# A linear attention followed by two Strassen MLPs: a new instruction order, and the ninth key block's products on half-array tiles

## The chip, the cores and the metric

The kernel runs on one core of a Trainium2 chip. The metric is the device time of one execution in microseconds (us); lower is better. TensorE (PE) multiplies matrices, VectorE (DVE) and ScalarE (ACT) work element by element, GpSimd (POOL) helps them, and SyncE (SP) issues the loads and stores. PEld is the loading of TensorE's stationary operand.

## The reference, cut to what matters

```
def phi(x):                                   # batch 4, heads 8, seq 576, head_dim 64, d_feat 128
    proj = einsum('bhsd,df->bhsf', x, w_phi)
    proj = proj - max(abs(proj), axis=-1, keepdims=True)
    return concatenate([exp(proj), exp(-proj)], axis=-1)
q_p, k_p = phi(q), phi(k)
kv  = einsum('bhsf,bhsd->bhfd', k_p, v);  z = sum(k_p, axis=2)
out = einsum('bhsf,bhfd->bhsd', q_p, kv) / (einsum('bhsf,bhf->bhs', q_p, z)[..., None] + 1e-6)
x = out as [2304, 512]
h = x @ w_in   (512 x 2048);  x = elu(h) @ w_out        # first MLP
h = x @ w_in2; x = (h * clip(h + 3, 0, 6) / 6) @ w_out2 # second MLP
```

Weights come as 64-bit floats. All matrix products keep close to fp32.

## The kernel before

**Attention.** Eight units (u = 0 to 7) of two batches and two heads each. A unit's sequence is nine blocks of 64 rows per batch, r = 0 to 8. Its steps, by the names of the code:

- `PJ`: projections of k and q into PSUM banks `ps_p` (64 rows by 128 columns of the array, both row halves at work side by side). `PJk0` holds blocks 0 to 7 of k, `PJq0` those of q, `PJx8` block 8 of both.
- `MX` and `SB` on DVE: the largest magnitude (`mx`), and the shift by it (`shk`, `shq`, and `sh` for block 8). Each pair of `MX` and `SB` works on one bank.
- `EX` on ACT: exp and exp of the negative, tile `kp`.
- `KV` on PE: the products of `kp` with v into two banks `ps_a`. For whole blocks the array is cut into 128 rows by 64 columns, for block 8 (`KVx80`, `KVx81`) into four quarters of 64 by 64.
- `ST` on ACT: the copy `st` of `ps_a`.
- `QT`: transposes of `shq` into `ps_t` (64 by 128 tiles), `QE` on ACT: exp of those into `e`.
- `NM`: three groups of products of `e` with `st` into `ps_n` (128 by 64 tiles); `RT`, `RB` on DVE: divide, tile `nr`; `XT`: transposes of `nr` (64 by 128); `XC` on ACT: into `x`.

So TensorE's array changes its cut between steps: PJ, QT and XT share one, whole KV and NM another, block 8's KV has a third, the MLPs use the whole array.

**MLPs.** Sixteen weight groups g (eight of each MLP), each by Strassen's seven products `P1` to `P7` on two pairs of token blocks, the fifth block directly (`hid4`, L838), then the second matmul (`outp`, L891, bank `ps_y`). An operand is split into a high part and a remainder (`x_hi`, `x_lo`); the activation is `act1` (ACT, L858 and L859), `gate` (DVE, L865), `gate_hi` (ACT, L869) and `gate_lo` (DVE, L872) into tiles `ga` and `gb`. POOL, ACT and DVE turn the 64-bit weights into parts `w_in` and `w_out`.

**What sets the order.** No order is written down. Each step has a rank; `in_order` walks over all engines and takes, of the steps that could start within 0.3 us of the soonest, the one of lowest rank, with modelled durations. The rank of an attention step is its unit's due time, less the longest chain behind it, plus an entry of the table `BIAS`; that of an MLP step is its due time plus `SHIFT`. `ON_POOL` names the element-wise steps that POOL does instead of DVE. On PE the MLP steps keep their own sequence, and only where the attention ends may the two mix. `ROW_T` is the modelled time of one pair of transposes, `rows` names a step's cut of the array, and each change of it counts as `TURN` in the model.

Of the kernel before, what the change touches and what calls it, by code (L numbers as in the profile page):

```python
# [101 lines left out]
}  # L102
ON_POOL = """
a01S40 a01S41 a10S10 a10S21 a10S30 a11S10 a11S11 a11S20 a11S40 l00S40 l00S41 l01A111 l01S10
l01S20 l01S21 l01S30 l01S31 l01S40 l04x0 l10A220 l10S10 l10S21 l11A220 l11S21 l11S31 l14x1 l14x3
""".split()


class Token:


    def __init__(self, ring):
# [3 lines left out]
class Step:  # L116
    def __init__(self, engine, us, fn, after=(), rank=0.0, takes=(), uses=(), port=False, behind=(), rows=128):
# [5 lines left out]
        self.lag = LATENCY[engine]  # L123


LAG = {"PE": 0.18, "DVE": 0.10, "ACT": 0.12, "POOL": 0.12, "SP": 2.2, "NONE": 0.0}
LATENCY = {"PE": 0.25, "DVE": 0.11, "ACT": 0.14, "POOL": 0.12, "SP": 2.2, "NONE": 0.0}
WINDOW = 0.3
ROW_T = 0.112
IN_BANKS = ("p", "a0", "a1", "t", "h", "y")  # L130
PORT = 0.05


def in_order(steps, rings):

# [108 lines left out]
def attention_then_two_mlps(  # L244
# [29 lines left out]
    NF = w_phi.shape[1]  # L274
# [72 lines left out]
    XC = {}  # L347
    last = {}

    def unit(u):  # L350
# [13 lines left out]
        Tk = {}  # L364
# [926 lines left out]
```

## Time and profile before

| | |
|---|---|
| median of 3 runs | 913.4 us (912.88 to 913.46) |
| the profiled execution | 910.73 us, span of its instructions 909.0 us |
| TensorE busy | 887.3 us, 98% of the span, in 7,018 matmul records |
| VectorE, ScalarE, GpSimd busy | 653.0 us (72%), 568.0 us (62%), 406.2 us (45%) |
| mean granted TensorE clock | 0.998 of 2.4 GHz |

The span runs from the first instruction to the last. A share of busy time is a mean over stages: the attention takes about the first 160 us, the MLPs the rest. An fp32 matmul of the attention shows as two records, a transpose as one.

### The profile page before, as it was taken

What the parts mean: (1) busy time and instruction counts of PE and PEld (TensorE: products, weight loads), DVE (VectorE), ACT (ScalarE), POOL (GpSimd) and SP (SyncE); (2) the same over time, 40 slices, a digit from 0 to 9 for tenths busy, and PEclk for the clock granted to TensorE, in tenths of its full rate; (3) what the DMA queues carried; (4) which work ended last, traced back from release to release, by engine and by line L of the source; (5) the groups of instructions that cost most, each with busy time, mean ns of one, the idle gap of its engine ahead of it and who ended that gap; (6) DMA issues with size and microseconds to landing.
All of it is one profiled execution on the core that took longest, in us unless ns stands there. A gap on an engine that the chain in (4) does not pass through costs nothing.

```text
span 909.0 us, 18043 instructions
## 1 busy us (share of the span) xinstructions
PE 887.3 (98%) x7018; PEld 756.8 (83%) x7018; DVE 653.0 (72%) x1197; ACT 568.0 (62%) x1215; POOL 406.2 (45%) x577
## 2 busy tenths in 40 slices
PE   8998998799999999999999999999999999999998
PEld 8888887688888888888888888888888888888887
DVE  6888887645767676767677897576767676667655
ACT  5886877868666565656566878765545454545331
POOL 0357523624545353535352676745444444444200
PEclk9999999999999999999999999999999999999999
DMA  8534511001111111111111101111111111110013
GB/s 249 154 115 119 143 38 37 1 1 47 47 60 35 58 36 58 35 58 36 58 35 48 47 1 47 59 58 58 48 58 47 48 42 51 35 59 24 0 70 140
DMA packets 42678, 53.66 MB, mean 59 GB/s; under 512 B 21344, under 2 KB 21728, under 8 KB 42592
## 3 DMA queue, kind: packets, MB, share of 16 engines
q1 hardware_dynamic: 42448, 52.44, 18.6%
q8 instruction: 55, 0.90, 0.4%
q14 instruction: 31, 0.25, 0.1%
q10 hardware_dynamic: 144, 0.07, 0.0%
HBM read 47.78 MB, written 4.72 MB: 58 GB/s over the span
## 4 chain that ended last, share of the span: by engine, by line
PE 90%; DVE 8%; ACT 1%; issue 0%; DVEq 0%
PE ps_y L891 43%; PE ps_h L824 33%; PE ps_h L838 5%; DVE mx L432 3%; PE ps_p L422 3%; PE ps_n L537 2%; DVE shq L446 2%; PE ps_a L484 1%; DVE nr L550 1%; PE ps_t L498 1%; DVE shk L446 1%; ACT e L515 0%; PE ps_w L332 0%; DVE dn L546 0%; DVE w_a L761 0%
## 5 line engine op out<-in xcount | busy, mean ns | idle before, releaser
L907 DVE TENSOR_TENSOR x<-ps_y,x 128x512 f32<-128x512 f32 (+1 forms) x267 | 175.3, 660 | 87.0 <-PE ps_y L891 84.1
L824 PE MATMUL ps_h<-x_S,w_in 128*128 128x512 f32 x768 | 190.1, 390 | 1.6 <-ACT mb L846 1.6
L824 PEld LDWEIGHTS ps_h<-x_S,w_in 128*128 128x128 f32 x768 | 143.8, 188 | 31.9 <-ACT mb L846 2.2
L824 PE MATMUL ps_h<-x_A,w_in 128*128 128x512 f32 x576 | 143.6, 390 | 0.0
L782 POOL TENSOR_TENSOR w_in<-w_bi,w_in 128x256 fp32r<-128x256 f32 x128 | 95.9, 766 | 78.7 <-ACT w_in L778 78.0
L824 PEld LDWEIGHTS ps_h<-x_A,w_in 128*128 128x128 f32 x576 | 107.2, 188 | 21.7
L891 PE MATMUL ps_y<-gb,w_out 128*128 128x512 f32 (+1 forms) x576 | 118.7, 354 | 0.0
L891 PE MATMUL ps_y<-w_out,gb 128*128 128x512 f32 (+1 forms) x486 | 117.5, 386 | 0.0
L891 PEld LDWEIGHTS ps_y<-gb,w_out 128*128 128x128 f32 x576 | 97.0, 189 | 16.1
L891 PEld LDWEIGHTS ps_y<-w_out,gb 128*128 128x128 f32 x486 | 90.5, 188 | 18.6
L765 POOL TENSOR_TENSOR w_bi<-w_bi,w_a 128x256 int32<-128x256 int32 x64 | 48.0, 754 | 122.5 <-DVE w_a L761 122.5
L749 POOL TENSOR_SCALAR w_a<-w_a 128x256 f32<-128x256 f32 x128 | 53.5, 419 | 103.4 <-ACT w_a L744 98.3
L891 PE MATMUL ps_y<-ga,w_out 128*128 128x512 f32 x384 | 94.5, 395 | 3.3 <-ACT ga L869 3.3
L891 PE MATMUL ps_y<-w_out,ga 128*128 128x512 f32 x384 | 92.3, 390 | 0.0
L891 PEld LDWEIGHTS ps_y<-ga,w_out 128*128 128x128 f32 x384 | 72.2, 191 | 18.2 <-ACT ga L869 3.7
L891 PEld LDWEIGHTS ps_y<-w_out,ga 128*128 128x128 f32 x384 | 71.2, 188 | 14.2
L765 POOL TENSOR_TENSOR w_bo<-w_bo,w_a 128x256 int32<-128x256 int32 x64 | 48.2, 755 | 68.4 <-DVE w_a L761 68.4
L865 DVE SCALAR_TENSOR_TENSOR ps_h<-ma,ps_h 128x512 f32<-128x512 f32 x80 | 55.4, 693 | 30.0 <-ACT ma L861 16.5
L851 DVE TENSOR_TENSOR ps_h<-ps_h,mb 128x512 f32<-128x512 f32 x64 | 44.6, 697 | 41.8 <-ACT w_a L744 20.0
L846 ACT COPY mb<-ps_h 128x512 f32<-128x512 f32 x64 | 37.7, 588 | 58.2 <-PE ps_h L824 57.8
L791 POOL TENSOR_TENSOR w_out<-w_bo,w_out 128x256 fp32r<-128x256 f32 x64 | 48.2, 752 | 51.6 <-ACT w_out L787 51.0
L872 DVE TENSOR_TENSOR gb<-ps_h,gb 128x512 fp32r<-128x512 f32 x80 | 54.5, 685 | 9.7 <-ACT gb L869 9.6
(80 smaller groups left out, 1460.4 us busy)
## 6 DMA issues: line engine op xcount, KB each, us to landing
w<-in_moe_w_in_dram SPq DMA_DIRECT2D x64, 256.0 KB, 2.6
w<-in_moe_w_out_dram SPq DMA_DIRECT2D x64, 256.0 KB, 2.6
vb<-in_v_dram SPq DMA_DIRECT2D x16, 288.0 KB, 4.9
out_dram<-x SPq DMA_DIRECT2D x17, 256.0 KB, 2.0
raw_k<-in_k_dram SPq DMA_DIRECT2D x7, 576.0 KB, 4.7
raw_q<-in_q_dram SPq DMA_DIRECT2D x7, 576.0 KB, 4.8
raw_k<-in_k_dram SPq DMA_DIRECT2D x1, 320.0 KB, 4.6
raw_q<-in_q_dram SPq DMA_DIRECT2D x1, 320.0 KB, 5.0
```

The costliest lines, as they stand in the source:

```text
L749: nc.gpsimd.tensor_scalar(out=st["a"], in0=st["a"], scalar1=W_MOST, scalar2=W_LEAST, op0=ALU.min, op1=ALU.max)
L765: nc.gpsimd.tensor_tensor(out=b_, in0=b_, in1=st["a"].bitcast(I32), op=ALU.add)
L782: nc.gpsimd.tensor_tensor(out=t[:, 1], in0=F[key], in1=t[:, 0].bitcast(F32), op=ALU.subtract)
L791: nc.gpsimd.tensor_tensor(out=t[:, 1], in0=F.pop((m, w, 1, c)), in1=t[:, 0].bitcast(F32), op=ALU.subtract)
L824: nc.tensor.matmul(out=PS[ps_], lhsT=t[:, a_, kk], rhs=X[pr, op][x_][kk], start=(opens and i == 0), stop=(i == 5), skip_group_check=True,)
L838: nc.tensor.matmul(out=PS[ps_][:, 256 * fi:256 * fi + 256], lhsT=t[:, a_, kk], rhs=XB["x"][x_][2 * half + kk], start=(i == 0), stop=(i == ...
L846: nc.scalar.copy(out=MAIN[key], in_=PS[ps_])
L851: V.tensor_tensor(out=PS[to], in0=PS[ps_], in1=MAIN[key], op=ALU.add)
L865: V.scalar_tensor_tensor(out=PS[ps_], in0=MAIN[key], scalar=s, in1=PS[ps_], op0=o0, op1=o1)
L872: V.tensor_tensor(out=GG[key][:, 1], in0=PS.pop(ps_), in1=GG[key][:, 0].bitcast(F32), op=ALU.subtract)
L891: nc.tensor.matmul(out=o, lhsT=a_, rhs=b_, start=(fi + j == 0), stop=(fi == 1 and j == 2),)
L907: V.tensor_tensor(out=part, in0=ps, in1=part, op=ALU.add)
```

## The change

All entries of `BIAS`, `SHIFT` and `ON_POOL` are replaced, `ROW_T` goes from 0.112 to 0.057, and the products of block 8 are issued as 64 rows by 128 columns: one matmul of 128 columns for two of 64, with the same `rows` number as projections and transposes.

```diff
 BIAS = {
-    "EX": 5.9, "EXk00@0": -17.4, "EXk00@7": 2.9, "EXk01@0": 15.2, "EXk10": 7.8, "EXx80": 44.2,
...
+    "EX": -2252.3, "EXk00": -2202.0, "EXk00@0": -2258.0, "EXk00@7": -2241.4, "EXk01": -2272.9,
...
 ON_POOL = """
-a01S40 a01S41 a10S10 a10S21 a10S30 a11S10 a11S11 a11S20 a11S40 l00S40 l00S41 l01A111 l01S10
-l01S20 l01S21 l01S30 l01S31 l01S40 l04x0 l10A220 l10S10 l10S21 l11A220 l11S21 l11S31 l14x1 l14x3
+a01S11 a01S31 a01S41 a10S11 a10S20 a10S30 a11S11 l00S40 l00S41 l01A110 l01S31 l04x0 l04x1 l04x2
+l10A111 l10S10 l10S21 l11A110 l11A111 l11A121 l11S11 l11S30 l14x1 l14x2
 """.split()
...
-ROW_T = 0.112
+ROW_T = 0.057
...
                 for half in range(2):
-                    for f0 in (0, 64):
+                    for f in (slice(0, NF),) if r == 8 else (slice(0, 64), slice(64, NF)):
                         for bb, p in parts:
                             nc.tensor.matmul(
-                                out=acc[bb][f0:f0 + 64, h, half], lhsT=kp[p, i, half, f0:f0 + 64],
+                                out=acc[bb][f, h, half], lhsT=kp[p, i, half, f],
...
-                    uses=[tk, Tk["v"], Tk["acc", 0], Tk["acc", 1]], rows=65 if j == "x8" else 66)
+                    uses=[tk, Tk["v"], Tk["acc", 0], Tk["acc", 1]], rows=64 if j == "x8" else 66)
```

Line numbers of the changed kernel are 16 higher from here on. What the tables do is seen in the order of instructions.

**Inside a unit, TensorE.** From the last `NM` of one unit to the first of the next. `ps_t` from `nr` is XT, from `shq` and `sh` QT; `kp_2016` and `kp_1961` are block 8. Before:

```order
L537 MATMUL ps_n_2095<-st,e 64x65 x24
L498 MATMUL ps_t_2134<-ident,nr 128x64
...
L484 MATMUL ps_a_2166<-vb_108,kp_2016 64x65
...
L422 MATMUL ps_p_2204<-wphi,raw_q 128x128
...
L484 MATMUL ps_a_2166<-vb_108,kp 64x65 x16
L484 MATMUL ps_a_2167<-vb_108,kp 64x65 x16
L498 MATMUL ps_t_2276<-ident,shq 128x64
...
L484 MATMUL ps_a_2167<-vb_108,kp_2016 64x65
...
L484 MATMUL ps_a_2167<-vb_108,kp 64x65 x16
L498 MATMUL ps_t_2342<-ident,shq 128x64
...
L422 MATMUL ps_p_2386<-wphi,raw_k 128x128
```

In the changed kernel:

```order
L553 MATMUL ps_n_2036<-st,e 64x65 x24
L514 MATMUL ps_t_2077<-ident,nr 128x64
...
L438 MATMUL ps_p_2095<-wphi,raw_q 128x128
...
L514 MATMUL ps_t_2128<-ident,nr 128x64
...
L500 MATMUL ps_a_2144<-vb_108,kp 64x65 x32
L514 MATMUL ps_t_2190<-ident,shq 128x64
...
L500 MATMUL ps_a_2144<-vb_108,kp_1961 128x65
...
L500 MATMUL ps_a_2145<-vb_108,kp 64x65 x32
L514 MATMUL ps_t_2285<-ident,shq 128x64
...
L438 MATMUL ps_p_2319<-wphi,raw_k 128x128
```

The projections of q now stand between XT1 and XT2 (`ps_t_2077` takes 12 transposes, `ps_t_2128` the last six), the whole KV products come in twos, and block 8's products stand among transposes. The cut of the array changes 6 times from one unit's NM to the next, 10 times before (units 3 to 6); up to the first `ps_y` it changes 57 times instead of 90.

**Inside a unit, VectorE.** The maxima and shifts of q's four banks. Before:

```order
L432 TENSOR_REDUCE mx<-ps_p_1815 128x4
L446 TENSOR_TENSOR shq<-ps_p_1815,mx 128x512
L432 TENSOR_REDUCE mx<-ps_p_1816 128x4
L446 TENSOR_TENSOR shq<-ps_p_1816,mx 128x512
L432 TENSOR_REDUCE mx<-ps_p_1805 128x4
L446 TENSOR_TENSOR shq<-ps_p_1805,mx 128x512
```

In the changed kernel:

```order
L448 TENSOR_REDUCE mx<-ps_p_1725 128x4
L448 TENSOR_REDUCE mx<-ps_p_1726 128x4
L462 TENSOR_TENSOR shq<-ps_p_1725,mx 128x512
L462 TENSOR_TENSOR shq<-ps_p_1726,mx 128x512
L448 TENSOR_REDUCE mx<-ps_p_1716 128x4
L771 SCALAR_TENSOR_TENSOR w_bo<-w_1479,w_bo 128x256
```

A shift followed its own maximum at once in eight places of a unit; in the changed kernel other work stands between the two in all but one or two.

**Where the MLP begins, TensorE.** Unit 7's last transposes of q and the first Strassen products (`ps_h`). Before:

```order
L824 MATMUL ps_h_3150<-x_A_0_113,w_in 128x512 x6
L824 MATMUL ps_h_3161<-x_A_0_114,w_in 128x512 x6
L824 MATMUL ps_h_3173<-x_S_0_117,w_in 128x512 x6
L498 MATMUL ps_t_3109<-ident,shq 128x64
...
L537 MATMUL ps_n_3204<-st,e 64x65 x24
```

In the changed kernel:

```order
L514 MATMUL ps_t_3039<-ident,shq 128x64
...
L840 MATMUL ps_h_3067<-x_A_0_113,w_in 128x512 x6
L840 MATMUL ps_h_3081<-x_A_0_114,w_in 128x512 x6
L553 MATMUL ps_n_3092<-st,e 64x65 x24
...
L840 MATMUL ps_h_3214<-x_S_0_117,w_in 128x512 x6
```

All of q's transposes now stand ahead of the first two Strassen products; the third product went behind NM.

**Where the MLP begins, ScalarE.** The activation of the tile that the first `ps_y` takes second (`ps_h_3150` before, `ps_h_3067` in the changed kernel), from its `act1` to its `gate_hi`. Before:

```order
L858 ACTIVATE ma<-ps_h_3150 128x512
L859 ACTIVATE ma<-ma 128x512
L807 CAST x_S_1_3352<-x_63 128x512
...
L858 ACTIVATE ma<-ps_h_3387 128x512
...
L869 CAST gb<-ps_h_3372 128x512
L858 ACTIVATE mb<-ps_h_3173 128x512
...
L869 CAST ga<-ps_h_3150 128x512
```

In the changed kernel:

```order
L874 ACTIVATE ma<-ps_h_3067 128x512
L875 ACTIVATE ma<-ma 128x512
L885 CAST gb<-ps_h_3287 128x512
L823 CAST x_S_1_3253<-x_63 128x512
L885 CAST ga<-ps_h_3067 128x512
```

Two instructions stand between the tile's activation and its `ga` instead of nine. From the first `ps_y` to the end TensorE's 3,492 matmuls come in the same sequence as before.

## Rows read from the trace of the kernel before

**Rows 1.** Stretches: length; busy time (instructions) of PE, PEld, DVE, ACT, POOL; clock; DMA; GB/s

```profile
99.55:117.58 18.03, 16.72 (x430) 15.38 (x430) 15.54 (x34) 12.98 (x33) 4.20 (x7) 1.00 0.36 98
172.00:175.00 3.00, 2.93 (x7) 2.32 (x8) 2.95 (x4) 2.12 (x5) 2.57 (x2) 0.50 0.00 0
190.00:880.00 690.00, 690.00 (x3302) 581.96 (x3301) 487.06 (x874) 422.04 (x880) 325.24 (x472) 1.00 0.14 44
```

**Rows 2.** Waits of TensorE, whole span: us in total, times, longest

```profile
PE ps_t L498 <- DVE shq L446: 5.9, 10, 1.7
PE ps_t L498 <- DVE nr L550: 3.6, 5, 0.7
PE ps_y L891 <- ACT ga L869: 3.3, 1, 3.3
PE ps_h L824 <- ACT mb L846: 1.6, 2, 1.3
PE ps_n L537 <- ACT e L515: 1.5, 3, 0.7
```

**Rows 3.** TensorE in order of time, one unit: start, us, records, [idle before]

```profile
99.88 1.54 PE L484 MATMUL ps_a<-vb,kp 128*64 128x65 f32 x48
...
103.34 2.09 PE L484 MATMUL ps_a<-vb,kp 128*64 128x65 f32 x64
105.36 0.46 PE L498 MATMUL ps_t<-ident,shq 64*128 64x64 f32 x8
...
109.43 0.41 PE L498 MATMUL ps_t<-ident,shq 64*128 64x64 f32 x8
109.68 2.01 PE L422 MATMUL ps_p<-wphi,raw_k 64*128 64x128 f32 x32
...
117.58 0.40 PE L498 MATMUL ps_t<-ident,nr 64*128 64x64 f32 x6 [0.71 <-DVE nr L550]
117.91 1.54 PE L484 MATMUL ps_a<-vb,kp 128*64 128x65 f32 x48
```

**Rows 4.** TensorE in order of time: one whole KV step, and block 8's

```profile
45.52 1.15 PE L484 MATMUL ps_a<-vb,kp 128*64 128x65 f32 x32
...
136.95 0.70 PE L484 MATMUL ps_a<-vb,kp 64*64 64x65 f32 x32
137.58 2.06 PE L422 MATMUL ps_p<-wphi,raw_q 64*128 64x128 f32 x32
```

**Rows 5.** VectorE in order of time, q's maxima and shifts

```profile
104.78 0.68 DVE L432 TENSOR_REDUCE mx<-ps_p 128x4 f32<-128x512 f32 x1
105.49 0.69 DVE L446 TENSOR_TENSOR shq<-ps_p,mx 128x512 f32<-128x512 f32 x1
106.10 0.68 DVE L432 TENSOR_REDUCE mx<-ps_p 128x4 f32<-128x512 f32 x1
```

**Rows 6.** Loads of the stationary operand by shape, 27 to 160 us: busy, mean ns

```profile
L484 PEld LDWEIGHTS ps_a<-vb,kp 128*64 128x64 f32 x896 | 28.0, 138 | 2.4 <-ACT kp L455 0.6
...
L498 PEld LDWEIGHTS ps_t<-ident,shq 64*128 64x128 f32 x224 | 9.4, 138 | 6.9 <-DVE shq L446 3.9 <-issue 1.1 <-PE ps_t L498 0.5
```

**Rows 7.** TensorE in order of time, the first matmuls into ps_y

```profile
172.07 5.24 PE L891 MATMUL ps_y<-ga,w_out 128*128 128x512 f32 x15 [3.28 <-ACT ga L869]
177.15 2.88 PE L824 MATMUL ps_h<-x_A,w_in 128*128 128x512 f32 x12
179.87 1.52 PE L891 MATMUL ps_y<-ga,w_out 128*128 128x512 f32 x6
```

**Rows 8.** ScalarE in order of time, ahead of the first ps_y

```profile
165.37 0.63 ACT L859 ACTIVATE ma<-ma 128x512 f32<-128x512 f32 x1
...
168.13 0.60 ACT L858 ACTIVATE ma<-ps_h 128x512 f32<-128x512 f32 x1 [0.80 <-PE ps_h L838]
...
171.44 0.58 ACT L869 CAST ga<-ps_h 128x512 fp32r<-128x512 f32 x1
```

**Rows 9.** DMA issues by line: KB each, median us to landing

```profile
raw_k<-in_k_dram SPq DMA_DIRECT2D x7, 576.0 KB, 4.7
```

152 rows, old and new, of tables (BIAS, SHIFT) are left out of this document.

## The prediction, on record before the changed kernel ran

> **What bounds the kernel now.** I read the stretches first: from 190 to 880 us TensorE is busy for all of the 690 us at full clock [rows 1], and its sequence from the first `ps_y` on is not changed, so nothing is won there. What can move is the time at which this stretch begins. Next the waits of TensorE [rows 2]: 16 us in these five kinds, none of them behind the start of `ps_y`. Then one unit in order of time [rows 3]: from one whole-block KV to the same step a unit later it takes 117.91 - 99.88 = 18.03 us. In that time TensorE is busy for 16.72 and VectorE for 15.54 [rows 1]: TensorE is nearest the bound, VectorE is close behind, and each stops the other in turn. At the entry of the MLP one stop of 3.28 us stands [rows 7], and behind it the clock is 0.50 of 2.4 GHz, the lower level, over the whole stretch from 172 to 175 us [rows 1].
>
> The sum is made against the profiled execution: 910.73 us, of which 909.0 are the span and 1.7 lie around it. It is 2.7 us below the median of 913.4. About 0.2% (1.8 us) is what a measurement of this kernel can tell from no change.
>
> **Changes of the array's cut.** A whole-block KV step with 64 records occupies TensorE from 103.34 to 105.36, 2.02 us [rows 3]. 32 more records cost 2.09 - 1.15 = 0.94 [rows 3, 4], so the 64 alone are 1.88, and 0.14 is left for one change of cut. The order has 33 fewer of them up to the first `ps_y`: **-4.6 us**. They count in full only where TensorE then doesn't wait longer; that is the first rival.
>
> **Block 8's products.** Now 32 records, two steps, take 137.58 - 136.95 = 0.63, less one change of cut 0.49, or 0.245 a step [rows 4]. Afterwards a step has four matmuls of two records, in side-by-side pairs: four pairs. No row has this shape. The nearest has the same cut, the same stationary width of 128 columns and 64 moving columns for 65: eight transposes, four pairs, from 109.43 to 109.68, 0.25 us [rows 3]. A far bound is the projection with 128 moving columns: 32 records, 16 pairs, in 2.01 - 0.2 = 1.8, or 0.45 for four pairs [rows 3]. I take the transposes' 0.25: 16 steps by +0.005, **+0.1 us**; the bounds are 0 and +3.3. That 64 matmuls fewer are issued gives nothing, since four ran at once and now two do.
>
> Against this part of the change stands a possible doubling of the weight load. A load of 64 columns has a mean of 138 ns, one of 128 columns for the transposes 138 ns too [rows 6], and the latter are followed by their matmuls at the 0.25 for four pairs above. The Trainium skill's page "TensorE: Matmul & The Clock Gate", section "LDWEIGHTS (loading the stationary operand)", has a load's time grow with its columns, which at its figure is 107 ns for 128 and 53 for 64; if a pair could not be faster than its load, 64 pairs at 107 ns would by that page cost 3 us more, as an estimate. The trace differs, with its equal means of 138 ns, so I stay with +0.1.
>
> **The transposes of `nr`.** Five stops of about 0.71, 3.6 us together [rows 2], come before XT2, which stands right behind XT1: VectorE's divide of the third NM group is not done (117.58 [rows 3]). In six units, 1 to 6, the projections of q now stand in between, some 1.8 us; in unit 7 a Strassen product does. Unit 0 keeps its order and its stop. A stop costs a little beside the counted wait, since that is counted from the end of the last matmul: eight transposes that stop take 0.46 [rows 3], in a run 0.25, and part of the difference is a change of cut; I take 0.15. Four stops go: 4 x (0.71 + 0.15) = **-3.4 us**.
>
> **The transposes of q.** Ten stops for the shift of q, 5.9 us; one of 1.7 is the start and I leave it [rows 2]. Nine are left, 4.2 us and 9 x 0.15, together 5.6. Two things shorten them. XT2 (a fifth of a microsecond) and a change of cut stand between the projections of q and QT. And VectorE gets through faster: a shift right behind its maximum starts 105.49 - 104.78 = 0.71 after it, the next, independent maximum 0.61 after that [rows 5]. With six of eight such neighbours parted, a unit's VectorE work falls by 0.6, to about 15.0 us. But the second shift of a pair comes later for the first QT, and a stop of one kind may become one of another. I take half: **-2.8 us**, with 0 and -5.6 as bounds.
>
> A steady unit then takes 18.03 - 4 x 0.14 - 0.86 - 0.4 = 16.2 us, with VectorE at 15.0 of it, 93%: tight, not impossible.
>
> **The entry of the MLP.** Unit 7's last four transposes of q now come ahead of the first two Strassen products, not behind three. Those two (2.7 us, half of the 179.87 - 177.15 = 2.72 for 12 records is one) hide ScalarE's exp, for which NM waited 1.5 us in three stops [rows 2]: -1.5 - 3 x 0.15 = **-2.0 us**. The stop ahead of `ps_y`: the tile's activation is done at 166.0, its `ga` starts only at 171.44 [rows 8], because ScalarE has first to wait for the fifth block's product (168.13) and work off nine instructions. With two short casts in between, `ga` comes some 2 us after the activation, under the Strassen product and the fifth block's products, which TensorE still has to do: **-3.4 us** with the 0.15. And with no idle stretch of that size the clock has no reason to fall: 15 matmuls took 177.15 - 172.07 = 5.08, against 15 x 2.72/12 = 3.40 at the upper level [rows 7]: **-1.7 us**. The waits for ScalarE's copies `mb`, 1.6 us [rows 2], stay: P6, P5 and P3 follow each other more closely now, with the third product gone from ahead of NM; I add **+0.4 us**.
>
> **What costs nothing.** Three element-wise steps come to VectorE from GpSimd, at 0.7 us 2 us in all if uncovered; in the MLPs VectorE is busy for 487 of 690 us, ScalarE for 422 and GpSimd for 325 [rows 1], so TensorE covers them. The loads go out in nearly the same order behind the same buffers; a k load lands in 4.7 us [rows 9], a quarter of a unit. At the start all projections of unit 0 stand ahead of the first KV; its stop of 1.7 can go or double, and I take 0.
>
> **The sum.** -4.6 + 0.1 - 3.4 - 2.8 - 2.0 - 3.4 - 1.7 + 0.4 = -17.4. The profiled execution comes to 910.73 - 17.4 = 893.3, the median to 913.4 - 17.4 = **896.0 us**.
>
> **Rivals.**
> - *VectorE becomes the bound.* Then the shorter array work turns into longer stops and a unit takes 17.2, say, instead of 16.2: six units give back 6 us, and at the far end all of the first and fourth term, 7.4. For it: 15.54 busy of 18.03 already. Against: VectorE's own order saves 0.6. Time 902 to 904.
> - *New waits within the MLPs.* All their helper steps have new places. One stop of 0.7 us, the size of today's largest regular one, in each of 15 later weight groups costs 10 us: 906. Against: today there is no such stop in 690 us, with every helper below three quarters.
> - *Slower.* The MLP begins 15 us sooner, while GpSimd's conversion of weights begins no sooner. If a group then waits like today's first `ps_y`, it pays 3.4 for the stop and 1.7 for the clock, 5.1 us; from four such groups on (20.4 against 17.4) the kernel is slower, with five it is 921. Against: GpSimd has 365 of the 690 us free.
> - *The waits form anew.* If each stop refills what a change of cut gave, attention and entry together move nothing: 913.
>
> **How the numbers follow.** The forecast with its bounds (892 to 900, from both halves of the q stops and the start) has 0.72, VectorE as bound 0.17, waits in the MLPs 0.06, slower 0.03, nothing 0.02. The range of 892 to 905 takes in the first two and leaves out some 0.15. Faster: 0.72 + 0.17 + 0.06 = 0.95, of which I keep 0.94; same 0.02; slower 0.04.
>
> **What would show it.** Block 8's products: 64 by 128 tiles, pairs every 60 to 65 ns (112 if the far bound holds). Stops for `nr`: one or two instead of five, for q's shift at most six. A steady unit of 16.0 to 16.5 us. The first `ps_y` near 156.4 (172.07 less the terms ahead of it), without the stop, and the clock at 1.00 there. No TensorE wait behind it. The prediction is wrong if VectorE fills its unit, if the clock falls elsewhere, or if TensorE stops between 160 and 860 us.

## The result, and the profile after

The changed kernel takes 898.17 us (median of 6 runs, 897.28 to 899.46) where the kernel before beside it takes 913.43 (6 runs, 910.77 to 916.27): a ratio of 0.9833, 95% interval 0.9813 to 0.9852, faster by 1.7%. The time lies in the predicted range, 2.2 us above the predicted 896.0. The profiled execution takes 897.79 us with a span of 895.9, so against the 909.0 of before the span falls by 13.1 us, not by 17.4. The medians lie 15.3 apart. The profile of before is one of its faster executions: in 51 runs of the kernel before, its mean granted clock was 0.998, as in the profile, in only 14 (median 911.39), and 0.993 to 0.996 in 37 (913.5); in ten of the changed kernel it was 0.998 to 1.000.

First the stretches, as in [rows 1]: one unit (from unit 1's first NM to unit 2's), and the stretch in which the clock had fallen.

```profile
39.82:56.74 16.92, 15.94 (x417) 15.21 (x415) 15.05 (x34) 13.76 (x36) 7.82 (x11) 1.00 0.47 139
172.00:175.00 3.00, 3.00 (x15) 2.49 (x14) 1.10 (x3) 2.27 (x7) 1.60 (x3) 1.00 0.19 64
190.00:880.00 690.00, 688.69 (x3271) 579.32 (x3270) 489.81 (x870) 414.09 (x863) 316.34 (x462) 1.00 0.14 45
```

The clock stays at 1.00. A unit is shorter, but not 16.2 us. The first NM of units 1 and 6, before (lines L537) and after (the one of unit 1 after stands further down):

```profile
38.91 4.74 PE L537 MATMUL ps_n<-st,e 128*64 128x65 f32 x144
130.02 4.49 PE L537 MATMUL ps_n<-st,e 128*64 128x65 f32 x144
123.92 0.33 PE L553 MATMUL ps_n<-st,e 128*64 128x65 f32 x2
```

So five units take 91.11 us before and 123.92 - 39.82 = 84.10 after, 18.22 and 16.82 each. VectorE is still busy for 15.05 of 16.92. TensorE now idles for 1.3 us within the MLPs.

TensorE's waits over the whole span, as in [rows 2]: us in total, times, longest.

```profile
PE ps_t L514 <- DVE nr L566: 3.2, 6, 0.8
PE ps_t L514 <- DVE shq L462: 2.0, 5, 0.7
PE ps_h L840 <- ACT mb L862: 1.4, 2, 0.7
...
PE ps_h L854 <- POOL x_b L826: 0.8, 1, 0.8
...
PE ps_n L553 <- ACT e L531: 0.6, 4, 0.2
...
PE ps_y L907 <- DVE ga L888: 0.5, 1, 0.5
```

The stops for `shq` fell from 5.9 to 2.0, those for `e` from 1.5 to 0.6, the 3.3 for ScalarE's `ga` are gone. Of the 5.9, 1.7 was the stop at the start, where one of 0.6 stands now; the other nine, 4.2 us, became four of 1.35. Those for `nr` stayed: 3.2 us in six stops for 3.6 in five. The waits for `x_b` and for VectorE's `ga`, in the MLPs after 400 us, are new, and so are those for `raw_q` (0.6) and `kp` (0.7) at the start.

TensorE in order of time over the same unit, as in [rows 3].

```profile
39.82 4.42 PE L553 MATMUL ps_n<-st,e 128*64 128x65 f32 x144
44.99 0.58 PE L514 MATMUL ps_t<-ident,nr 64*128 64x64 f32 x12 [0.75 <-DVE nr L566]
45.41 2.00 PE L438 MATMUL ps_p<-wphi,raw_q 64*128 64x128 f32 x32
47.26 0.34 PE L514 MATMUL ps_t<-ident,nr 64*128 64x64 f32 x6
47.55 2.09 PE L500 MATMUL ps_a<-vb,kp 128*64 128x65 f32 x64
49.83 0.97 PE L514 MATMUL ps_t<-ident,shq 64*128 64x64 f32 x16 [0.19 <-DVE shq L462]
```

XT2 (47.26) doesn't stop any more, as forecast; in unit 0, where the prediction left its stop, 0.47 remains. But now XT0 does, by 0.75 (44.99): the other five stops for `nr`, 2.7 us in units 0, 1, 3, 4 and 5, are all XT0's. VectorE in order of time at that point shows why:

```profile
43.32 0.56 DVE L566 TENSOR_TENSOR nr<-ps_n,dn 128x384 f32<-128x384 f32 x1
43.79 0.68 DVE L462 TENSOR_TENSOR shk<-ps_p,mx 128x512 f32<-128x512 f32 x1
44.39 0.55 DVE L566 TENSOR_TENSOR nr<-ps_n,dn 128x384 f32<-128x384 f32 x1
```

The first group's reciprocal was done at 42.3 already, but its divide comes last of these three, behind the second group's divide and a shift of k, and ends at 44.94; XT0 starts at 44.99.

One step of block 8 (8 records, among transposes), as in [rows 4]; all 16 steps, busy and mean ns; and the loads of the stationary operand by shape, as in [rows 6] (busy, mean ns).

```profile
33.50 0.63 PE L500 MATMUL ps_a<-vb,kp 64*128 64x65 f32 x8
33.95 0.43 PE L514 MATMUL ps_t<-ident,shq 64*128 64x64 f32 x8
```

```profile
L500 PE MATMUL ps_a<-vb,kp 64*128 64x65 f32 x128 | 8.8, 274 | 0.0
```

```profile
L438 PEld LDWEIGHTS ps_p<-wphi,raw_q 64*128 64x128 f32 x248 | 15.0, 188 | 0.0
L514 PEld LDWEIGHTS ps_t<-ident,shq 64*128 64x128 f32 x224 | 9.2, 139 | 3.5 <-ACT kp L471 1.6 <-DVE shq L462 1.3
L500 PEld LDWEIGHTS ps_a<-vb,kp 64*128 64x128 f32 x112 | 7.0, 189 | 0.0
```

A step takes 33.95 - 33.50 = 0.45, with no change of cut before or behind it: the far bound of the prediction (0.45), not the transposes' 0.25. A load for block 8 now takes 189 ns, as for the projections (188), though the transposes with as many columns keep 139.

Where the MLP begins, as in [rows 7] and [rows 8]: TensorE, then ScalarE.

```profile
158.46 4.27 PE L907 MATMUL ps_y<-ga,w_out 128*128 128x512 f32 x18
162.56 2.88 PE L840 MATMUL ps_h<-x_A,w_in 128*128 128x512 f32 x12
```

```profile
155.38 0.63 ACT L875 ACTIVATE ma<-ma 128x512 f32<-128x512 f32 x1
...
157.11 0.59 ACT L885 CAST ga<-ps_h 128x512 fp32r<-128x512 f32 x1
```

All 18 matmuls run at once. The Strassen products behind them start at 162.56 where they started at 177.15, 14.6 us sooner. Of this, unit 7's first NM brings 9.45 (150.71 before, 141.26 after).

### The profile page after: what moved, and what is told of

It reads as the page before. It is cut to its first block, busy times and chain, and to the rows that moved or that the text cites. A ratio compares the mean times of both kernels' runs of the same rounds, so it can differ in the third digit from the quotient of the medians.

```text
span 895.9 us, 17806 instructions
## 1 busy us (share of the span) xinstructions
PE 881.2 (98%) x6890; PEld 754.5 (84%) x6890; DVE 651.2 (73%) x1200; ACT 567.5 (63%) x1215; POOL 401.6 (45%) x574
## 4 chain that ended last, share of the span: by engine, by line
PE 91%; DVE 6%; ACT 1%; DMA 1%; issue 1%; POOL 0%; SPq 0%; DVEq 0%
PE ps_y L907 44%; PE ps_h L840 34%; PE ps_h L854 5%; PE ps_a L500 3%; PE ps_n L553 3%; PE ps_p L438 2%; PE ps_t L514 2%; DVE mx L448 1%; DVE shk L462 1%; DVE nr L566 1%; DVE shq L462 1%; DMA raw_q<-in_q_dram 1%; ACT e L531 0%; DVE x L923 0%; DVE x_S L826 0%
```

## The experiments

Theory A, the prediction's: TensorE's own work sets the length of a unit, and each stop and each product has a price of its own that adds up. Theory B: VectorE's work fills the unit, so a single cure on TensorE only moves the stop. What C and D stand for, each expectation says. A span is that of the profiled execution; the changed kernel's is 895.9, that of before 909.0. The start differs between executions of the same steps by up to 0.9 us: the first 16 records of the projections, ahead of everything that these edits touch, take 1.16 us in the changed kernel's profile and 2.08 in another.

```profile
3.91 1.16 PE L438 MATMUL ps_p<-wphi,raw_k 64*128 64x128 f32 x16
4.01 2.08 PE L442 MATMUL ps_p<-wphi,raw_k 64*128 64x128 f32 x16
```

(The second line is of the run "The first divide sooner".) So differences of span below 1 us say little, and the length of the five units, from unit 1's first NM to unit 6's, is given for each run on the attention; it is 84.10 in the changed kernel and 84.09 in a second profile of it.

**Block 8 in quarters again** (the changed kernel; the order stays).

```diff
-for f in (slice(0, NF),) if r == 8 else (slice(0, 64), slice(64, NF)):
+for f in (slice(0, 64), slice(64, NF)):
```

> The changed kernel in its own order, with block 8's products issued as quarters (64 by 64) again. Theory A (the half tile made block 8 dearer: a pair every 0.112 us instead of four matmuls every 0.058, so 16 steps cost 0.45 instead of 0.24): 16 x 0.21 = 3.4 us come back, plus 0.05 for each of the 16 or so changes of cut that leave it, and one or two more changes of cut per unit cost 8 to 12 x 0.14 = 1.1 to 1.7; net -2 to -3 us, span 893 to 894, kernel about 895.5. Theory B (TensorE waits for VectorE anyway, so shorter products only lengthen the stops): 0, span 895.9. Theory C (the changes of cut are what the new shape pays for): +1 to +2, span 897.

898.23 us (4 runs, ratio 0.9839, 0.9818 to 0.9859), span 895.3. The block is quicker:

```profile
L500 PE MATMUL ps_a<-vb,kp 64*64 64x65 f32 x256 | 6.0, 226 | 0.0
```

Over all eight units the quarters are busy for 6.0 us, the halves of the changed kernel for 8.8. The first `ps_y` starts at 157.82, 0.64 sooner, and the five units take 83.47, 0.63 less: three of the seven spans from one unit's NM to the next are 0.25 to 0.28 us shorter, the other four equal within 0.07. But the cut now changes 68 times up to the first `ps_y` instead of 57. By the prices, 16 steps of 0.20 less 11 changes of 0.14 are 1.7 us. From unit 0's first NM to unit 7's, 0.84 arrives (118.61 for 119.45) and TensorE's counted stops grow by 0.2. About half is paid out: more than theory B has it, less than A.

**Halves alone** (the kernel before, with only block 8 as 64 by 128).

```diff
-for f0 in (0, 64):
+for f in (slice(0, NF),) if r == 8 else (slice(0, 64), slice(64, NF)):
```

> The kernel before, in its own order and with its own tables, with block 8's products alone issued as 64 by 128. Two changes of cut fall away per unit (block 8 stands beside projections or transposes), 16 x 0.14 = -2.2. Theory A (dearer products): +3.4 to +4.3, net +1 to +2, span about 910.5. The prediction's price (0.25 a step, no dearer): -2.1, span about 907. Theory B (stops absorb all): 909.0 within 0.5.

911.45 us (12 runs, ratio 0.9993, 0.9979 to 1.0007), span 910.0, first `ps_y` 0.7 us later. All steps of block 8:

```profile
L484 PE MATMUL ps_a<-vb,kp 64*128 64x65 f32 x128 | 9.5, 275 | 0.0
```

9.5 us for 6.7 of busy time. The 0.7 is all there at unit 0's first NM (20.89 for 20.16), and 0.5 of it ahead of any product of block 8 (first transposes of q at 10.75 for 10.23). From there to unit 7's first NM both kernels take 130.6 us (the five units 91.24 for 91.11): the dearer products, 14 changes of cut fewer (76 for 90) and 0.9 us less of counted stops come out even. By itself the new geometry gains nothing; what it can give is the freedom to stand among transposes without a change of cut.

**33 columns** (the changed kernel; block 8's products are formed with 33 of the 65 columns of v and the sum, the rest is left out).

```diff
+cut = slice(0, 33) if r == 8 else slice(0, D + 1)
-    out=acc[bb][f, h, half], lhsT=kp[p, i, half, f], rhs=vb[u % 2][p, r, h], ...
+    out=acc[bb][f, h, half, cut], lhsT=kp[p, i, half, f], rhs=vb[u % 2][p, r, h, cut], ...
```

> The changed kernel with block 8's products on 33 of the 65 moving columns, so half of block 8's share in kv and all of it in z is left out. If the pace of block 8 is set by the load of 128 stationary columns, its pairs stay at 0.112 us and the time is that of the changed kernel, 898 (span 895.9). If it is set by the moving columns, the pairs come every 0.06 and 3 us are gained: span 893.

897.41 us (4 runs, ratio 0.9831, 0.9814 to 0.9848), span 896.1, five units 84.00.

```profile
L501 PE MATMUL ps_a<-vb,kp 64*128 64x33 f32 x128 | 8.6, 270 | 0.0
```

Half of the moving columns, and the block takes 8.6 us for 8.8. The moving side doesn't set its pace; the 128 stationary columns, whose loads take 189 ns, are what is left, and with 64 of them (the quarters) the block is quicker.

**The first divide sooner** (the changed kernel; on VectorE the divide of the first NM group, RB0, is moved right behind RT0).

```diff
-    return [out[i] for i in order]
+    out = [out[i] for i in order]
+    for s in [x for x in out if getattr(x, "name", "") == "RB0"]:
+        out.remove(s)
+        out.insert(out.index(s.after[0]) + 1, s)
+    return out
```

> The changed kernel with one VectorE step moved in each unit: the divide of the first NM group comes right behind its own reciprocal instead of behind a shift of k and the second group's divide. Theory A (the new stop of TensorE at XT0, 0.23 to 0.75 us in five units, is due to this order alone): these 2.7 us go, span 893. Theory B (VectorE's work of a unit is what binds, so the shift that was pushed back now stops the projections of q, which need its bank): the stop at XT0 goes, one of the same size stands at the projections, span 895.9 to 897.

897.56 us (4 runs, ratio 0.9828, 0.9807 to 0.9848), span 895.7. The waits, and a unit of TensorE's timeline:

```profile
PE ps_t L518 <- DVE shq L466: 2.3, 4, 1.1
...
PE ps_t L518 <- ACT x L586: 1.0, 2, 0.5
...
PE ps_t L518 <- DVE nr L570: 0.7, 1, 0.7
```

```profile
87.85 0.46 PE L518 MATMUL ps_t<-ident,shq 64*128 64x64 f32 x8 [1.15 <-DVE shq L466]
```

XT0 doesn't stop any more; the 0.7 left for `nr` is XT2's in unit 0. In units 1 and 4 XT2 now stops by 0.52 for ScalarE's copy `x`. In this unit, unit 3, the changed kernel stops three times, for 0.23 (`nr`), 0.25 (`shk`) and 0.28 (`shq`); here it stops once, for 1.15. That is theory B's picture, but this unit is the worst of seven: it is 0.5 us longer than in the changed kernel, units 1 and 4 are 0.5 shorter, unit 0 is 1.0 shorter. The span is only 0.2 us shorter because this execution starts 0.9 us late (first NM at 22.73 for 21.81). From there to unit 7's first NM it takes 118.30 us for 119.45, 1.15 less; the five units take 83.86, 0.24 less. Neither theory A's 2.7 us nor theory B's nothing came.

**Both** (quarters again and the first divide sooner), run twice.

> The changed kernel with block 8 back in four quarters and, on VectorE, the divide of each first NM group moved right behind the first step of its pair. Theory A (the pair's load time and the waits are separate prices that add up): the two edits alone gave -0.6 and -0.2 us of span, so together -0.8, span near 895.1, time near 897.0, and first ps_y near 157.6. Theory B (VectorE's work fills the unit, so any single cure only moves the stop): the same or less, span 895.3 to 895.9; units of NM starts between 16.5 and 17.0 us as in either alone. A result under 894.0 of span would speak against B: then the two cures had blocked each other.

896.99 us (4 runs, ratio 0.9814, 0.9792 to 0.9837), span 896.6 in an execution whose clock fell once in unit 0. Without a fall two runs took 895.4 and 896.1, so it was run again beside the changed kernel on one chip:

> The changed kernel as it is, on the same chip as the next one, to compare the two. Theory A and B: median 897 to 899, mean clock 1.000 or 0.999 in nearly all runs.

> The changed kernel with block 8 in quarters and the first divide moved, a second time, beside the changed kernel. If it is a better version, its runs at a mean clock of 1.000 lie 1.5 to 3 us under those of the changed kernel (895.4 and 896.1 were seen), and its median is under 897; if the gain is eaten by falls of the clock, half of its runs show 0.998 and lie near 898, no better than the changed kernel.

The changed kernel: 897.58 us (4 runs, ratio 0.9840, 0.9822 to 0.9858). Both edits: 897.81 (5 runs, ratio 0.9833, 0.9817 to 0.9849), and two runs at a mean clock of 1.000 took 896.6 and 897.5 where three of the changed kernel took 897.4 to 897.7. No better version is shown. The five units take 83.30 us both times, 0.80 less than in the changed kernel, about the sum of the two edits' 0.63 and 0.24. But both profiled executions have a fall of the clock in unit 0, and five of these nine runs are at a mean clock of 0.998, where one of ten of the changed kernel is: that is enough to eat the gain, as the last expectation allows. Why the clock falls there was not followed.

**A shorter maximum** (the changed kernel; the maximum is taken over 64 of the 128 features, the other half is left out).

```diff
-out=mx[:, :n], in_=P[j, h], axis=AX.X, op=ALU.max, ...
+out=mx[:, :n], in_=P[j, h][:, :, 0:64], axis=AX.X, op=ALU.max, ...
```

> The changed kernel with the maximum taken over 64 of the 128 features of each row: half of the maximum's reading is left out, so the values differ, and nothing else changes. VectorE's nine maxima of a unit, about 0.68 us each, should take about 0.35, so its work per unit falls by some 3 us from 15 of 17 us. Theory B (VectorE's work sets the length of a unit): the stops for nr (3.2 us) and shq (2.0 us) go to under 2 us together, units fall to 16.3 us or less, and the span falls by 3 to 6 us, to 890 to 893. Theory A (TensorE's own work sets the unit, and what is over is block 8's slower products): span within 1 us of 895.9.

893.48 us (4 runs, ratio 0.9776, 0.9758 to 0.9793), span 891.2. The same unit as above, and the largest waits of TensorE:

```profile
38.08:54.48 16.40, 15.65 (x417) 15.10 (x415) 12.88 (x33) 13.69 (x36) 7.82 (x11) 1.00 0.51 143
```

```profile
PE ps_t L514 <- DVE nr L566: 3.2, 6, 0.8
PE ps_h L840 <- ACT mb L862: 1.3, 2, 0.7
```

VectorE's work in the unit falls from 15.05 to 12.88 us, TensorE's instructions are the same, and the kernel gains 4.7 us of span. The five units take 81.42, 2.68 less, or 0.54 a unit for the 2.2 that VectorE is spared. The edit also shortens the way from a projection to its shift, and no run parts that from VectorE's load. The stops for `shq` are gone. Those for `nr` are all there, which B had not expected: they come from the order on VectorE, not from its load.

**A shorter maximum and the first divide sooner.**

> The changed kernel with both edits: the maximum over 64 of the 128 features (half of the maximum's reading is left out, values differ) and the divide of each first NM group moved right behind the first step of its pair. If VectorE's work is why the second edit alone only moved the stops (-0.2 us of span), then with VectorE relieved it pays in full: the nr stops go from 3.2 us to under 1, shq stays near 0, and the span falls from 891.2 to 888 to 889.5. If the stops for nr are a latency from NM to the transposes that no order shortens, they stay at 2 us or more and the span stays within 0.7 of 891.2.

891.62 us (4 runs, ratio 0.9769, 0.9754 to 0.9785), span 889.7.

```profile
PE ps_t L518 <- DVE nr L570: 0.7, 1, 0.7
```

The divide that gave 0.2 us of span before gives 1.5 now; 889.7 is a little above the range given. But most of the difference between 0.2 and 1.5 is the start, which was 0.9 us later with the divide moved there and is 0.35 sooner here. From unit 0's first NM to unit 7's the divide gives 1.10 (114.48 for 115.58) where it gave 1.15, and in the five units 0.52 where it gave 0.24. The medians are 1.86 us apart here, on two chips, and 0 to 0.6 there, and their runs have such starts in them too. So it isn't shown that a cure of TensorE's stops is paid out only with VectorE relieved. Five units take 80.90 us (37.16 to 118.06), 16.18 each, the length that was forecast for the changed kernel.

**The old MLP tables** (the changed kernel with SHIFT and ON_POOL of the kernel before; BIAS stays new).

```diff
-SHIFT = {"a00S10": -3.3, "a00S11": 3.2, ...
+SHIFT = the table of the kernel before
-ON_POOL = "a01S11 a01S31 a01S41 ...
+ON_POOL = "a01S40 a01S41 a10S10 ...
```

> The changed kernel with the tables SHIFT and ON_POOL of the kernel before (the new BIAS, block 8 as 64 by 128). Theory A (the attention's gain comes from BIAS, the entry's gain from the MLP steps' new order): unit 7's first NM starts within 3 us of the changed kernel's 141.26 (before: 150.71), but TensorE stops again ahead of the first ps_y for ga by 3 us or more, and the clock falls behind it; in all 8 to 14 us slower than the changed kernel, 906 to 912 us. Theory C (the entry gained only because the attention ended sooner): no stop over 1 us ahead of ps_y, time within 3 us of the changed kernel, 895 to 901.

911.65 us (10 runs, ratio 0.9972, 0.9959 to 0.9985), span 909.5. TensorE where the MLP begins, and the clock there:

```profile
144.83 4.42 PE L556 MATMUL ps_n<-st,e 128*64 128x65 f32 x144
```

```profile
164.54 1.94 PE L857 MATMUL ps_h<-x_b,w_in 128*128 128x256 f32 x14 [3.16 <-DVE x_b L829]
...
169.86 1.22 PE L910 MATMUL ps_y<-ga,w_out 128*128 128x512 f32 x2 [2.68 <-ACT ga L888]
172.91 5.00 PE L910 MATMUL ps_y<-ga,w_out 128*128 128x512 f32 x13 [1.82 <-DVE ga L891]
```

```profile
170.00:175.00 5.00, 3.18 (x7) 2.07 (x8) 4.47 (x7) 2.34 (x4) 3.17 (x4) 0.50 0.18 52
```

Unit 7 reaches its first NM at 144.83, 5.9 us before the kernel before does. Nothing of that is left at the Strassen products behind the first `ps_y` (177.75 for 177.15): three stops of 7.7 us and a fall of the clock stand in between. Theory A's 8 to 14 us are right (13.5 against the median of 898.17), its 3 us for unit 7 are passed by 0.6, and the stops are for `x_b` (3.16) as well as for `ga` (4.5).

**The new MLP tables alone** (the kernel before with the new SHIFT and ON_POOL).

> The kernel before (its BIAS, block 8 in four quarters) with the new SHIFT and ON_POOL: the MLP's new order on the old attention. Theory A (the two tables bring parts that add up): unit 7's first NM starts within 2 us of before's 150.71, the 3.28 us stop ahead of the first ps_y goes and the clock stays up there, and the span falls by 4 to 7 us, to 902 to 905. Theory D (the tables bring their gain together only, since the helper steps ahead of the first ps_y compete with the attention's own steps on VectorE and ScalarE): the stop only moves or the attention's end comes later, span within 2 us of 909.

910.93 us (10 runs, ratio 0.9980, 0.9971 to 0.9989), span 908.9. The waits:

```profile
PE ps_y L888 <- DVE ga L869: 1.9, 2, 1.4
PE ps_h L821 <- ACT x_A L804: 1.4, 1, 1.4
PE ps_y L888 <- ACT ga L866: 1.1, 1, 1.1
```

The stop of 3.28 us becomes stops of 1.1 and 1.4 for `ga`, with 1.4 for the operand `x_A` behind them. Up to the `ps_y` that `ga` feeds this run gains: the Strassen products behind the first `ps_y` start at 173.04 for 177.15, though unit 7's first NM comes 1.6 us later (152.28), and the clock doesn't fall there. Then 2.4 of these 4.1 us go at once, with stops of 1.4 and 0.4 for `x_A` within those products, and 1.3 more in the two stops that the changed kernel has in the MLPs too. Theory D: BIAS with block 8 alone brings 0.28%, the MLP's tables alone 0.20%, all together 1.7%.

**The entry's stop alone** (the kernel before; the gate, gate_hi and gate_lo of the tile that stops `ps_y` are moved right behind their predecessors).

```diff
+    for what in ("gate", "gate_hi", "gate_lo"):
+        s = at[what]
+        out.remove(s)
+        out.insert(out.index(s.after[0]) + 1, s)
```

> The kernel before with one edit: the gate, gate_hi and gate_lo of the tile that the first ps_y takes second are moved right behind their predecessors on VectorE and ScalarE. Theory A (the stop of 3.28 us and the fall of the clock behind it are one cause with the price of 3.4 + 1.7 us): the stop for ga goes under 1 us, the clock stays at 1.00 from 150 us on, and the span falls by 3.5 to 5.1 us to 904 to 905.5. Theory B (TensorE then waits for the next thing: ScalarE's copy of ps_y or the weights): another stop of 2 us or more within 15 us, and the span falls by less than 1.5 us.

911.12 us (10 runs, ratio 0.9974, 0.9960 to 0.9987); the profiled execution, the slowest of the ten, has a span of 911.1, with its clock down twice.

```profile
151.79 0.33 PE L543 MATMUL ps_n<-st,e 128*64 128x65 f32 x2 [0.68 <-ACT e L521]
152.76 0.34 PE L543 MATMUL ps_n<-st,e 128*64 128x65 f32 x4 [0.65 <-ACT e L521]
153.25 5.87 PE L543 MATMUL ps_n<-st,e 128*64 128x65 f32 x138 [0.15 <-ACT e L521]
...
170.57 4.27 PE L897 MATMUL ps_y<-ga,w_out 128*128 128x512 f32 x18
...
182.69 1.74 PE L830 MATMUL ps_h<-x_S,w_in 128*128 128x512 f32 x6 [2.42 <-ACT ma L852]
184.23 4.48 PE L897 MATMUL ps_y<-gb,w_out 128*128 128x512 f32 x12
```

The stop ahead of `ps_y` is gone, and 12 us later one of 2.42 stands, for ScalarE's copy `ma`, with a new fall of the clock behind it. The other fall, at 153 us, lies ahead of the moved steps. Theory B holds for the place of the stop. The median still gains a little, and two runs at a mean clock of 1.000 have spans of 907.1 and 907.3, 1.7 to 1.9 under 909.0: more than B's 1.5, far from A's 3.5.

## Why the prediction was right or wrong

**Right in sign, and at the entry in size.** The entry was forecast at -2.0 - 3.4 - 1.7 + 0.4 = -6.7. Measured: 14.6 us between the two starts of the same Strassen products, less what the attention brings. Unit 7's first NM came 9.45 sooner, of which 1.45 is the third product that went behind it (149.56 - 148.11 in the trace of before) and 0.68 the first stop for `e`; so 7.3 belong to the attention and 7.3 to the entry. But the reason given, two casts in place of nine instructions ahead of `ga`, is too narrow: with that alone the stop comes back 12 us later, and with either half of the tables alone the whole gain is about 2 us. The clock's term came as forecast, but its reason, that without an idle stretch of that size the clock doesn't fall, is not safe: with the entry's stop alone it fell behind stops of 0.68, 0.65 and 0.15 us. The new MLP tables alone do gain 4.1 us at this place, and lose them behind it. The runs show that the steps of this stretch have to be in time together, those of the attention and those of the MLP; which of them each gain needs was not tried one by one.

**Changes of cut, -4.6.** A row of the new order agrees with the price: a whole KV step with 64 records in unit 6 takes from 131.67 to 133.70, 2.03 us, less 1.88 leaves 0.15. That the 4.6 arrive in full was not tested by itself; of the quarters run's sum of cheaper products and 11 more changes, half arrived.

**Block 8, +0.1: wrong.** This term was mis-sized. The prediction took the transposes as the nearest row; the projections were. A step costs 0.45, not 0.245: 16 x 0.20 = +3.2 us of TensorE's time, the bound that was kept for the range. The rule of the Trainium skill that was weighed there ("TensorE: Matmul & The Clock Gate", "LDWEIGHTS (loading the stationary operand)") was right in direction and near in size: 3 us more by its figure. The pairs agree with its 107 ns, one every 0.112 us; the loads' own rows are longer than its 107 and 53 ns. The equal means of 138 ns [rows 6] had compared a product with a transpose; with the same kind of matmul the load grows from 134 ns for 64 columns (the quarters run) to 189 for 128.

**The stops for `nr`, -3.4: wrong.** XT2's stops went as said. The step that failed is the silence on XT0: the prediction looked at what stands ahead of XT2 on TensorE and not at where the first divide now stands on VectorE. A stop stands there now, 2.7 us in five. That the order makes it is shown twice: moving the divide takes it away, and taking VectorE's load away doesn't.

**The stops for `shq`, -2.8: somewhat too little.** 3.9 us of the 5.9 went, but 1.1 of that is the stop at the start, which the prediction left out. Of the nine others 2.85 us went, with five stops fewer; at the prediction's 0.15 a stop that is 3.6.

**The steady unit.** 16.2 was forecast, 16.82 is the mean of five, a gain of 1.40 for 1.83. By the prices, block 8 takes 2 x 0.20 of it and the new stops at XT0 0.39 a unit, and the stops for the shift of q give back more than forecast; that is a sum, and the runs bear it out in part. The quarters run gains 0.13 a unit, half of the 2 x 0.20 - 0.14 that its products and one more change of cut come to. The first rival, VectorE as the bound, held in part too: with 2.2 us less for VectorE in a unit, and nothing else changed, a unit is 0.54 shorter. It isn't the whole bound: in the unit shown above VectorE itself waits for TensorE, for 0.63 and 0.78 us (before 42.89 and 54.52). Each stops the other in turn, as the prediction said of the kernel before, but at places that its sum didn't name. The 15.0 of 16.2 us that were called tight, not impossible, were not reached: a mean of 16.2 over the five units came only with the shorter maximum.

**Small terms.** The start, taken as 0, costs about 0.5: the first NM starts at 21.81 for 20.16, but there it was split and ended at 25.99, here it ends at 26.47. "No TensorE wait behind it" was wrong by 1.3 us, two stops in the MLPs. The rival with 0.7 in each of 15 groups and the slow entry of weights did not come; the waits that form anew came for `nr` alone.

**The median.** The sum was taken from the profile and from the median alike, 893.3 and 896.0. The profile missed by 4.5 us, the median by 2.2. The difference is no merit: the profiled execution of before had its clock down once, most of its runs were at a lower mean clock, and the change removed that too. A profile 2.7 us under its median asked for a reason, and the prediction gave none. There is luck in the 4.5 too: block 8, XT0 and the MLPs' two stops cost 3.2 + 2.7 + 1.3 = 7.2 us that the sum didn't have, and some of that was offset: by the stops for `shq` (0.8) and the entry (0.6), which came out better, and by 1 to 2 us that no row accounts for.

**What stays open.** How the 7.3 us of the attention divide over cuts, block 8 and stops was not taken apart. For two edits the parts do add up in the five units (0.63 and 0.24 alone, 0.80 together); whether those of the change do was not tested. How much of e's and `ga`'s stops each single table entry removed was not tried.

## What to carry to other kernels

Compare small edits over a stretch that begins and ends inside the kernel: the spans of single executions hold starts that differ by up to 0.9 us, and an edit worth 1.15 us looked like one worth 0.2. Where two engines are each busy for over 85% of a stage, take load off the other one once, to see how much of an edit's price can come in. When a stop is said to go, follow the late instruction on its producer's queue, not only what stands ahead of the consumer, and name the transfer or product that waits next. When an operand's shape has no row, take the row of the same operation with that operand's width, not one of another operation that shares the tile.

## What was not expected of the hardware

A pair of fp32 products with 128 stationary columns on 64 rows comes every 0.112 us, with 65 moving columns; with 33 the block's 128 records take 8.6 us for 8.8. Its loads take 188 to 189 ns; transposes with the same cut and the same 128 columns keep 138 to 139 ns a load, and four pairs run in 0.25 us [rows 3]. What makes the transposes cheaper was not tried.

The clock fell where no long stop preceded it. In the run with the entry's stop alone, TensorE waited for `e` for 0.68, 0.65 and 0.15 us and then took 5.87 us for 138 records, where the kernel before with the same instructions and the same three stops took 4.30; the granted clocks over 153 to 156.5 us were

```profile
153.00:156.50 3.50, 3.35 (x67) 3.25 (x65) 1.37 (x4) 2.42 (x5) 1.28 (x1) 0.57 0.00 0
```

and, in the kernel before,

```profile
153.00:156.50 3.50, 3.50 (x120) 3.43 (x118) 2.83 (x8) 1.34 (x3) 0.98 (x1) 1.00 0.02 5
```

The moved steps come later, so the edit didn't cause it. 0.57 lies between the two levels, so most of that stretch went at the lower one, 1.2 GHz. Three of the falls cost nearly the same: 5.87 - 4.30 = 1.57 here, 4.48 - 2.88 = 1.60 behind the stop of 2.42, 5.08 - 3.40 = 1.68 behind the 3.28 of before.
